# Top-k attention followed by a GELU MLP: the first MLP block over two slots, whole blocks from slot 12 on, and another order of the first loads

## The chip, the cores and the metric

The kernel runs on one core of one Trainium2 chip. A core has five engines that run side by side, each with its own stream of instructions: TensorE (matmuls; PE in the profile, with PEld for the loads of its stationary operand), VectorE (DVE), ScalarE (ACT), GpSimd (POOL) and SyncE (SP, which here only issues transfers). The metric is device time in microseconds (us), the median of several runs.

## The reference

```python
# q, k, v: (8, 8, 576, 64): 8 batches, 8 heads, 576 rows, 64 columns
scores = q @ k^T / sqrt(64)
kth    = 32nd largest score of each row
scores = where(scores >= kth, scores, -1e9)
attn   = softmax(scores)                 # over what is left; 1e-9 in the denominator
x      = (attn @ v), heads side by side  # (4608, 512)
out    = gelu(x @ w_in) @ w_out          # w_in (512, 2048), w_out (2048, 512), exact GELU
```

All of it is fp32.

## The kernel before

Two heads make a *pair*; 128 rows of a pair make an *item* (a last item of each two pairs takes the 64 rows that are left of each). There are 144 items. The main loop has a *slot* for each: in slot n the kernel starts the scores of item n+2, works on the softmax of item n-1, on the transposes of item n-2, on the product with v of item n-3, and searches the 32 largest of each row of item n.

```python
ahead = N + 4                                   # N = 144
for n in range(ahead):
    left[0] = 7 if START < n < START + 2 * NP else 8     # START = 10, NP = 4: pieces of the MLP in this slot
    weights_add(unit_in(n))                     # GpSimd: second half of a weight conversion
    scores(n + 2)                               # TensorE, and evictions by ScalarE
    product = attend(n - 3)                     # TensorE: attn @ v for two items, in every second slot
    late = n > START
    mlp(1)                                      # one piece, if its tokens are ready and left[0] > 0
    tr = transposes(n - 2)                      # TensorE, and copies by ScalarE
    ...
    softmax(n - 1, 0)                           # ScalarE: Prelu, then Exp with its sum, first half
    mlp(1)
    if not late:
        softmax(n - 1, 1)
    mlp(1)
    ...                                         # pieces between the transposes and those of later q and k
    if late:
        softmax(n - 1, 1)
    add_small(n - 1)                            # GpSimd: den + 1e-9
    ...
    run_gelus()
    mlp(left[0])                                # the pieces that are left
    run_gelus()
    if n < N:
        top_k(n, {3: lambda: inverse(n - 1)})   # VectorE: 4 rounds of MAX8 and MATCH_REPLACE8; 1/den at its end
    threshold(n)                                # GpSimd
    u = unit_in(n + 1)
    normalise(n - 1, 0 if u not in words else 2 if on_pool(u) else 1)  # halves done by VectorE, the others by GpSimd
    weights_size(unit_in(n + 1))                # ScalarE: first half of a weight conversion
    if n >= FIRST:
        load_weights(n + 2)
```

The MLP runs in *pieces*: L1 (x @ w_in) and L2 (gelu @ w_out), eight pieces to a *block* of two units, L1 and L2 blocks in turn. A unit of L1 fills one PSUM buffer, of which there are two; GELU empties it. The two GELUs of an L1 block are put in line after its last piece (first block) or after the sixth piece of the L2 block that follows, and run at the next `run_gelus`, at the latest ahead of the first piece of an L1 unit.

```python
def l1_piece(u, x):
    ...
    if x == 0:
        run_gelus()
    for ko in range(part * KO // m, (part + 1) * KO // m):
        nc.tensor.matmul(h_tile(u)[:, i, :], lhsT=w_in_sb[...], rhs=xT[...], ...)

GELU_AT = 5
pieces += behind(block(0, True), 7, (0, 1)) + block(2, True)
for u in range(2, NU, 2):
    pieces += behind(block(u - 2, False), GELU_AT, (u, u + 1))
    if u + 2 < NU:
        pieces += block(u + 2, True)
```

The weights come in as doubles whose words are converted to fp32 on the chip, in 16 units, one in a slot (the last two are a slot apart): two or three ScalarE operations of 128x1024 elements, and two or three of GpSimd. Units that fall in a slot before `START` take three on ScalarE, those from `START` on take their third on GpSimd (`on_pool`). Where a unit is converted, VectorE takes one or both halves of the normalisation from GpSimd.

```python
ORDER = [0, 1, 2, 3, 8, 9, 4, 5, 10, 11, 6, 7, 12, 13, 14, 15]
FIRST = 1
START = 2 * NP + 2
WARM = 16
SLOT_OF = {u: FIRST + i + (i == UNITS - 1) for i, u in enumerate(ORDER)}
```

The start: memsets, first loads, matmuls that only keep TensorE busy (`warm`), then the transposes of the first two pairs and the scores of items 0 and 1.

```python
for n, ts in raws.items():
    for t in ts[: 1 if n == "v" else 2]:
        (nc.vector if n == "v" else nc.gpsimd).memset(t[:, NM], 0.0)
make_identity(nc, ident)
for t in raws["v"][1:]:
    nc.gpsimd.memset(t[:, NM], 0.0)
...
load("k", 0, nc.scalar, nc.gpsimd)     # main part by ScalarE's queue, the 64 last rows by GpSimd's
load("q", 0)                           # all others by SyncE's queue
load("k", 1)
load("q", 1)
for n in range(2):
    load_weights(FIRST + n)
idle = raws["v"][0][:, NM].rearrange("p e d -> p (e d)")
warm = ps.tile([P, 512], f32, tag="l1", name="warm")
for _ in range(WARM):
    nc.tensor.matmul(warm[:, 0:P], lhsT=idle, rhs=idle, start=True, stop=True)
for pair in range(2):
    for piece in transpose_qk(pair, pair == 0):
        piece()
    if pair == 0:
        scores(0)
        scores(1)
```

The eviction of an item's scores, in `scores(i)`:

```python
nc.scalar.activation(spread(s, S + TL, SM), s_ps, func=AF.Copy, scale=scale)        # 128 x 1024
nc.scalar.activation(s[:, SM : S + TL], t_ps[:, 0:P], func=AF.Copy, scale=scale)    # 128 x 128
```

Of the kernel before, what the change touches and what calls it, by code (L numbers as in the profile page):

```python
# [14 lines left out]
def kernel(  # L15
# [19 lines left out]
    nc = tc.nc  # L35
    f32, i32, u32 = mybir.dt.float32, mybir.dt.int32, mybir.dt.uint32
    bf16, i16, u16 = mybir.dt.bfloat16, mybir.dt.int16, mybir.dt.uint16
    AF = mybir.ActivationFunctionType
    ALU = mybir.AluOpType

    B, H, S, D = q.shape
    P = 128
# [3 lines left out]
    NP = H // 2  # L46
    NM = S // P
    SM = NM * P
    TL = S - SM
# [6 lines left out]
    scale = 1.0 / float(D) ** 0.5  # L56
# [8 lines left out]
    ident = const.tile([P, P], f32, name="ident")  # L65
# [4 lines left out]

    raws = {n: [const.tile([P, NJ, 2, D], f32, name=f"raw_{n}{i}") for i in range(m)]
            for n, m in (("k", 2), ("q", 2), ("v", NP + 1))}
    for n, ts in raws.items():
        for t in ts[: 1 if n == "v" else 2]:
            (nc.vector if n == "v" else nc.gpsimd).memset(t[:, NM], 0.0)
    make_identity(nc, ident)
    for t in raws["v"][1:]:
        nc.gpsimd.memset(t[:, NM], 0.0)


    n_pairs = B * NP
# [2 lines left out]
    def raw_of(n, pair):  # L84
        return raws[n][pair % len(raws[n])]

    def load(n, pair, queue=None, queue2=None):
        if pair >= n_pairs:
            return
        queue = queue or nc.sync  # L90
        queue2 = queue2 or queue
        b, h0 = pair // NP, 2 * (pair % NP)
        t, src = raw_of(n, pair), sources[n]
        for e in range(2):
            queue.dma_start(
                out=t[:, 0:NM, e, :], in_=src[b, h0 + e, 0:SM].rearrange("(t p) d -> p t d", p=P)
            )
            queue2.dma_start(out=t[e * TL : (e + 1) * TL, NM, e, :], in_=src[b, h0 + e, SM:S])

# [18 lines left out]


    ORDER = [0, 1, 2, 3, 8, 9, 4, 5, 10, 11, 6, 7, 12, 13, 14, 15]
    FIRST = 1
    START = 2 * NP + 2
    WARM = 16
    words = {}
    low = const.tile([P, 1], f32, name="low")
    nc.gpsimd.memset(low, -EXP0 * 2.0**19)
# [3 lines left out]

    SLOT_OF = {u: FIRST + i + (i == UNITS - 1) for i, u in enumerate(ORDER)}
    UNIT_IN = {n: u for u, n in SLOT_OF.items()}
    unit_in = UNIT_IN.get
# [29 lines left out]
    def parts(u):  # L165

        t, dst = words[u], weights_of(u)[3].bitcast(i32)
        return t[:, :, 0::2], t.bitcast(mybir.dt.int16)[:, :, 2::4], t[:, :, 1::2].bitcast(i32), dst

    def weights_size(u):  # L170
        if u not in words:
            return
        w, first, below, d = parts(u)
        nc.scalar.activation(d, first, func=AF.Relu, bias=low, scale=2.0**19)

        nc.scalar.activation(below, first, func=AF.Prelu, bias=high, scale=2.0**-21, alpha=2.0**40)
        if not on_pool(u):
            nc.scalar.activation(w.bitcast(i32), w.bitcast(u32), func=AF.Copy, scale=2.0**-13)

    def on_pool(u):  # L180

        return SLOT_OF[u] >= START
# [3 lines left out]
    def weights_add(u):  # L186
        if u in words:
            w, _, below, d = parts(u)
            if on_pool(u):
                nc.gpsimd.tensor_scalar(  # L190
                    w.bitcast(i32), w.bitcast(u32), 2.0**-13, None, op0=ALU.mult
                )
            nc.gpsimd.tensor_tensor(d, d, below, op=ALU.add)
            nc.gpsimd.tensor_tensor(d, d, w.bitcast(i32), op=ALU.add)
        made.add(u)
# [53 lines left out]
    def spread(t, step, n):  # L249

        return bass.AP(tensor=t.tensor, offset=t.offset, ap=[list(t.ap[0]), [step, 2], [1, n]])

    def half(r, e):


        return slice((r ^ e) * TL, ((r ^ e) + 1) * TL)
# [5 lines left out]
    def scores(i):  # L262
        if i >= N:
            return
        pair, t = items[i]
        S_of[i] = s = work.tile([P, 2 * S], f32, tag="s", bufs=5, name="s")
        s_ps = ps.tile([P, 2, 512], f32, tag="s", bufs=1, name="s_ps")
        t_ps = ps.tile([P, 512], f32, tag="tp", name="t_ps")
        if t < NM:
            qk = qk_of[pair]  # L270
            lhsT = qk[:, t * P : (t + 1) * P]
            nc.tensor.matmul(t_ps[:, 0:P], lhsT=lhsT, rhs=qk[:, SM + P : KT], start=True, stop=True)  # L272
            for c in range(2):
                for e in range(2):
                    rows = slice(e * D, (e + 1) * D)
                    nc.tensor.matmul(  # L276
                        s_ps[:, e, c * 256 : (c + 1) * 256], lhsT=lhsT[rows, :],
                        rhs=qk[rows, KT + c * 256 : KT + (c + 1) * 256], start=True, stop=True,
                    )
            nc.scalar.activation(spread(s, S + TL, SM), s_ps, func=AF.Copy, scale=scale)  # L280
            nc.scalar.activation(s[:, SM : S + TL], t_ps[:, 0:P], func=AF.Copy, scale=scale)  # L281
        else:
            for r in range(2):
                qk = qk_of[pair + r]
                for e in range(2):
                    nc.tensor.matmul(
                        t_ps[half(r, e), r * TL : (r + 1) * TL],
                        lhsT=qk[:, SM + e * TL : SM + (e + 1) * TL],
                        rhs=qk[:, SM + P + e * TL : SM + P + (e + 1) * TL],
                        start=True, stop=True,  # L290
                    )

            for r in range(2):
                qk = qk_of[pair + r]
                for e in range(2):
                    rows = slice(e * D, (e + 1) * D)
                    nc.tensor.matmul(  # L297
                        s_ps[half(r, e), r, :], lhsT=qk[rows, SM + e * TL : SM + (e + 1) * TL],
                        rhs=qk[rows, KT:], start=True, stop=True,
                    )  # L300
            s2 = s.rearrange("p (r n) -> p r n", r=2)
            nc.scalar.activation(s2[:, :, 0:SM], s_ps, func=AF.Copy, scale=scale)
            nc.scalar.activation(
                s2[:, :, SM:S], t_ps[:, 0:P].rearrange("p (r n) -> p r n", r=2),
                func=AF.Copy, scale=scale,
            )
# [44 lines left out]
    def add_small(i):  # L351
        if i < 0 or i >= N:
            return
        st = stat_of[i]
        nc.gpsimd.tensor_scalar(st["den"], st["den"], 1e-9, None, op0=ALU.add)  # L355
# [224 lines left out]
    ready, left = [0], [0]  # L580
    staging = ExitStack()
    stage = staging.enter_context(tc.tile_pool(name="stage", bufs=1))

    load("k", 0, nc.scalar, nc.gpsimd)
    load("q", 0)
    load("k", 1)
    load("q", 1)
    for n in range(2):
# [10 lines that stand above are left out]
        if pair == 0:  # L599
            scores(0)  # L600
            scores(1)

# [10 lines left out]
    ahead = N + 4  # L615
    for n in range(ahead):

        left[0] = 7 if START < n < START + 2 * NP else 8
        weights_add(unit_in(n))
        scores(n + 2)  # L620
        product = attend(n - 3)
        late = n > START
        mlp(1)
        tr = transposes(n - 2)
        if product and n > START and done[0] < len(pieces) and pieces[done[0]][0] > ready[0]:

            for piece in tr[:1]:
                piece()
            tr, ready[0] = tr[1:], n_tok[0]
        softmax(n - 1, 0)  # L630
# [4 lines that stand above are left out]
        prep = prep_in.pop(n, [])  # L635
        if len(prep) > 1 and len(tr) == 3:
            tr, prep = tr[:1] + prep[:1] + tr[1:], prep[1:]
        for piece in tr[:-1]:
            piece()
            ready[0] = n_tok[0]  # L640
            mlp(1)
        ready[0] = n_tok[0]
        if late:
            softmax(n - 1, 1)
        add_small(n - 1)
        for piece in tr[-1:] + prep:
# [4 lines that stand above are left out]
        mlp(left[0])  # L651
        run_gelus()
        if n < N:
            top_k(n, {3: lambda: inverse(n - 1)})
        else:
            inverse(n - 1)
        threshold(n)
        u = unit_in(n + 1)

        normalise(n - 1, 0 if u not in words else 2 if on_pool(u) else 1)  # L660

        weights_size(unit_in(n + 1))
        if n >= FIRST:
            load_weights(n + 2)
        if n <= NP:
            load("v", n)
# [38 lines left out]
```

## Time and profile before

| | before |
|---|---|
| median of 3 runs | 1654.69 us (1654.48 to 1655.39) |
| profiled execution, first to last instruction | 1653.7 us |
| VectorE's first MAX8 (search of item 0) | 13.09 us |
| start of the search of items 10 and 11 | 115.87 and 126.64 us |
| start of the search of item 18 | 209.82 us |
| slowest of its instructions, in total: MAX8 and MATCH_REPLACE8 | 1152 and 864 of about 0.74 us each |
| GpSimd's normalisation of one half, 128x576 | 1.72 us |

The profile is that of one execution. Its page gives the busy time of each engine, then the span in 40 equal slices with a digit for the busy tenths, then the transfers, the chain of work that ended last, and the costliest groups. A line of a group, or of the instructions in order of time, names the engine, the line of the kernel, the operation, and output and inputs by the program's names; in square brackets stands how long the engine had been idle before it, and what released it. A slot has no mark in the profile; it can be told on TensorE by its score matmuls (`t_ps`, then `s_ps`), and on VectorE by the first MAX8 on `s`. An fp32 matmul shows as two instructions, a transpose as one.

### The profile page before, as it was taken

To read this page: it belongs to the slowest core of one execution; us is meant where nothing else is said; L and a number is where in the kernel's file an instruction comes from. 1 tells how busy PE (TensorE), PEld (TensorE's weight loads), DVE (VectorE), ACT (ScalarE), POOL (GpSimd) and SP (SyncE) were. 2 spreads that over 40 slices of the span, in tenths; PEclk is the share of its full clock that TensorE was granted. 3 is DMA by queue.
4 is the path that set the end of the run, shared out by engine and by line. 5 is a ranking of instruction groups with operands and counts; after the bars stand their busy time and mean duration, and the time that the engine had idled before them with its cause. 6 is when DMAs were issued, how large, how long until landed. Compare 5 with 4: busy or idle time off the path is not lost.

```text
span 1653.7 us, 25056 instructions
## 1 busy us (share of the span) xinstructions
PE 1593.8 (96%) x8832; PEld 1080.5 (65%) x8832; DVE 1419.6 (86%) x3049; ACT 1184.1 (72%) x2131; POOL 650.5 (39%) x756
## 2 busy tenths in 40 slices
PE   6669999999999999999999999999999999999999
PEld 4346566766666667676666667676666666666665
DVE  7999899989999889998989988998889898999800
ACT  6888777777777777777777777777777777777720
POOL 3677543333333333333333333333333333333300
PEclk7669999999999999999999999999999999999999
DMA  6423210011101111011110111001110001000000
GB/s 165 139 98 102 83 43 1 14 29 29 50 1 28 30 30 28 1 28 36 29 28 1 42 29 43 1 14 28 44 35 1 27 15 34 2 14 4 4 13 13
DMA packets 126621, 56.14 MB, mean 34 GB/s; under 512 B 117760, under 2 KB 117792, under 8 KB 126496
## 3 DMA queue, kind: packets, MB, share of 16 engines
q1 hardware_dynamic: 125376, 54.25, 12.2%
q8 instruction: 70, 1.15, 0.3%
q14 instruction: 55, 0.45, 0.1%
q10 hardware_dynamic: 1056, 0.26, 0.1%
q0 software_dynamic: 64, 0.03, 0.0%
HBM read 45.08 MB, written 9.44 MB: 33 GB/s over the span
## 4 chain that ended last, share of the span: by engine, by line
PE 92%; ACT 6%; DVE 1%; issue 1%; POOL 0%; ACTq 0%; POOLq 0%; DVEq 0%
PE h_ps L495 30%; PE y_ps L531 30%; PE o L443 9%; PE s_ps L276 8%; PE tp L412 8%; PE tp_qk L231 2%; PE t_ps L272 2%; ACT s L363 1%; PE o L454 1%; ACT s L362 1%; PE s_ps L297 1%; PE tp_t L394 1%; ACT s L280 1%; POOL s L375 0%; PE warm L595 0%
## 5 line engine op out<-in xcount | busy, mean ns | idle before, releaser
L323 DVE MAX8 top<-rest 128x8 f32<-128x576 f32 x864 | 608.9, 746 | 0.0
L495 PE MATMUL h_ps<-xT,w_in_sb 128*128 128x256 f32 (+1 forms) x2560 | 554.5, 362 | 3.8 <-ACT g L506 3.8
L531 PE MATMUL y_ps<-w_out_sb,g 128*128 128x512 f32 x1152 | 549.5, 599 | 0.0
L495 PEld LDWEIGHTS h_ps<-xT,w_in_sb 128*128 128x128 f32 x2560 | 429.6, 191 | 66.6 <-issue 19.6
L375 POOL TENSOR_SCALAR s<-s,rden 128x576 f32<-128x576 f32 x266 | 456.0, 1723 | 0.8 <-issue 0.4
L326 DVE MATCH_REPLACE8 rest<-top,rest 128x576 f32<-128x576 f32 x576 | 423.0, 741 | 0.0
L355 POOL TENSOR_SCALAR den<-den 128x2 f32<-128x2 f32 x144 | 32.0, 222 | 835.2 <-ACT s L363 834.4
L531 PEld LDWEIGHTS y_ps<-w_out_sb,g 128*128 128x128 f32 x1152 | 195.1, 190 | 166.8 <-issue 165.0
L280 ACT ACTIVATE s<-s_ps 128x1024 f32<-128x1024 f32 x128 | 131.5, 1027 | 167.3 <-PE s_ps L276 149.1
L363 ACT ACTIVATE s<-s,bias 128x576 f32<-128x576 f32 x288 | 223.3, 776 | 13.3 <-ACT s L362 0.7
L362 ACT ACTIVATE s<-s,neg 128x576 f32<-128x576 f32 x288 | 223.9, 778 | 0.3 <-POOL neg L338 0.2
L419 ACT COPY pt<-tp 128x512 f32<-128x512 f32 x256 | 147.1, 574 | 103.0 <-PE tp L412 103.0
L412 PEld LDWEIGHTS tp<-ident,s 128*128 128x128 f32 x1152 | 145.9, 144 | 111.9 <-issue 59.1
L326 DVE MATCH_REPLACE8 rest<-top,s 128x576 f32<-128x576 f32 x288 | 211.6, 742 | 0.0
L323 DVE MAX8 top<-s 128x8 f32<-128x576 f32 x288 | 201.8, 742 | 3.9 <-ACT s L281 3.9
L412 PE MATMUL tp<-ident,s 128*128 128x128 f32 x1152 | 178.6, 279 | 23.6 <-ACT pt L395 22.0
L443 PE MATMUL o<-pt,raw_v 128*64 128x256 f32 x1280 | 155.5, 390 | 0.0
L276 PE MATMUL s_ps<-qk 64*128 64x256 f32 x1024 | 153.9, 421 | 0.7 <-ACT s L280 0.7
L349 DVE RECIPROCAL rden<-den 128x2 f32<-128x2 f32 x144 | 23.0, 160 | 142.1 <-POOL den L355 141.8
L443 PEld LDWEIGHTS o<-pt,raw_v 128*64 128x64 f32 x1280 | 87.8, 139 | 66.2 <-issue 23.4
L276 PEld LDWEIGHTS s_ps<-qk 64*128 64x128 f32 x1024 | 92.5, 195 | 23.7 <-issue 1.6
L506 ACT ACTIVATE g<-h_ps 128x512 f32<-128x512 f32 x144 | 78.6, 595 | 34.0 <-PE h_ps L495 33.2
(66 smaller groups left out, 1088.3 us busy)
## 6 DMA issues: line engine op xcount, KB each, us to landing
raw_q<-in_q_dram SPq DMA_DIRECT2D x64, 128.0 KB, 2.4
raw_v<-in_v_dram SPq DMA_DIRECT2D x64, 128.0 KB, 2.5
out_dram<-y SPq DMA_DIRECT2D x32, 256.0 KB, 2.1
w_out_sb<-in_moe_w_in_dram SPq DMA_DIRECT2D x16, 511.8 KB, 4.9
raw_k<-in_k_dram SPq DMA_DIRECT2D x62, 128.0 KB, 2.5
w_out_sb<-in_moe_w_out_dram SPq DMA_DIRECT2D x10, 511.8 KB, 3.9
words<-in_moe_w_out_dram SPq DMA_DIRECT2D x6, 511.8 KB, 4.5
raw_q<-in_q_dram SPq DMA_DIRECT2D x64, 16.0 KB, 2.3
```

What stands on the lines that cost most here:

```text
L276: nc.tensor.matmul(s_ps[:, e, c * 256 : (c + 1) * 256], lhsT=lhsT[rows, :], rhs=qk[rows, KT + c * 256 : KT + (c + 1) * 256], start=True, s ...
L280: nc.scalar.activation(spread(s, S + TL, SM), s_ps, func=AF.Copy, scale=scale)
L323: nc.vector.max(st["top"][:, e, 8 * r : 8 * r + 8], cur[e])
L326: nc.vector.match_replace(rest[:, e], st["top"][:, e, 8 * r : 8 * r + 8], cur[e], LOWEST)
L362: nc.scalar.activation(s, s, func=AF.Prelu, bias=st["neg"][:, e, 1:2], scale=1.0, alpha=STEEP)
L363: nc.scalar.activation(s, s, func=AF.Exp, bias=st["bias"][:, e : e + 1], scale=1.0, accum_out=st["den"][:, e : e + 1],)
L375: (nc.vector if e >= 2 - on_dve else nc.gpsimd).tensor_scalar(s, s, st["rden"][:, e : e + 1], None, op0=ALU.mult)
L412: nc.tensor.transpose(tp[:, j * P : (j + 1) * P], s[:, first + j * P : first + (j + 1) * P], ident)
L419: nc.scalar.copy(out=dst, in_=tp.rearrange("p (j n) -> p j n", j=NM))
L443: nc.tensor.matmul(o[e * D : (e + 1) * D, 0:n], lhsT=vt[:, j, e, :], rhs=pt[:, e * NM + j if j < NM else 2 * NM, :], start=(j == 0), stop= ...
L495: nc.tensor.matmul(h_tile(u)[:, i, :], lhsT=w_in_sb[:, ko, f * P : (f + 1) * P], rhs=xT[:, ko, c0 : c0 + n], start=(ko == 0), stop=(ko == ...
L531: nc.tensor.matmul(y_of[sub], lhsT=g_of[u][:, i, sub * P : (sub + 1) * P], rhs=w_out_sb[:, f, :], start=(f == 0), stop=(f == FT - 1),)
```

## The change

The first L1 block of the MLP, which could run whole in slot 10, is spread over slots 10 and 11, four pieces in each; from slot 12 on each slot has eight pieces, so that a slot holds one whole block (before, seven pieces in slots 11 to 17). The conversion of the weights begins in slot 0 instead of slot 1, so each of the 16 units is there a slot earlier. At the start, the first k load is issued ahead of GpSimd's other work, most memsets go to VectorE, the first loads stand ahead of the identity's making, the warm-up has 9 matmuls instead of 16, and the scores of item 0 are evicted by ScalarE and VectorE together. The aim is an earlier first search, and slots that begin with a block of the MLP.

```diff
-    for n, ts in raws.items():
-        for t in ts[: 1 if n == "v" else 2]:
-            (nc.vector if n == "v" else nc.gpsimd).memset(t[:, NM], 0.0)
-    make_identity(nc, ident)
-    for t in raws["v"][1:]:
-        nc.gpsimd.memset(t[:, NM], 0.0)
+    nc.gpsimd.memset(raws["k"][0][:, NM], 0.0)
+    for t in raws["v"][:1] + raws["q"] + raws["k"][1:] + raws["v"][1:]:
+        nc.vector.memset(t[:, NM], 0.0)
@@ after the definition of load()
+    load("k", 0, nc.scalar, nc.gpsimd)
+    load("q", 0)
+    make_identity(nc, ident)
@@
-    FIRST = 1
+    FIRST = 0
     START = 2 * NP + 2
-    WARM = 16
+    WARM = 9
@@ scores(i)
+            if i == 0:
+                nc.scalar.activation(s[:, 0:SM], s_ps[:, 0], func=AF.Copy, scale=scale)
+                nc.vector.tensor_scalar(s[:, SM : S + TL], t_ps[:, 0:P], scale, None, op0=ALU.mult)
+                nc.vector.tensor_scalar(s[:, S + TL :], s_ps[:, 1], scale, None, op0=ALU.mult)
+                return
@@ ahead of the first transposes
-    load("k", 0, nc.scalar, nc.gpsimd)
-    load("q", 0)
     load("k", 1)
@@ behind the first transposes
             scores(0)
             scores(1)
+    weights_size(unit_in(FIRST))
@@ the main loop
-        left[0] = 7 if START < n < START + 2 * NP else 8
+        left[0] = 4 if n in (START, START + 1) else 8
```

## The prediction

> **What bounds the kernel now.** I read the page first (shares and slices), then cut the span into stages, then asked for the waits of the stage in which an engine is idle, and last for the instructions in order of time at the two places that the change touches.
>
> ```profile
> PE 1593.8 (96%) x8832; PEld 1080.5 (65%) x8832; DVE 1419.6 (86%) x3049; ACT 1184.1 (72%) x2131; POOL 650.5 (39%) x756
> ...
> PE   6669999999999999999999999999999999999999
> ...
> PEclk7669999999999999999999999999999999999999
> ```
>
> TensorE has the largest share, but the slices show two regimes: the first three slices (about 120 us) are not full, all others are. The stages in numbers (columns: span, length, busy us and instructions of PE, PEld, DVE, ACT, POOL, granted clock, DMA share, GB/s):
>
> ```profile
> 0.00:13.10 13.10, 10.11 (x56) 8.95 (x58) 1.20 (x4) 3.06 (x4) 3.37 (x19) 1.00 0.68 177
> 13.10:112.00 98.90, 58.42 (x276) 37.03 (x276) 98.40 (x211) 85.50 (x141) 63.15 (x53) 0.66 0.46 134
> 112.00:206.80 94.80, 86.46 (x467) 56.92 (x468) 84.67 (x183) 76.71 (x127) 64.47 (x47) 0.96 0.30 92
> 206.80:215.00 8.20, 5.16 (x38) 3.34 (x37) 8.20 (x20) 5.12 (x12) 5.23 (x6) 1.00 0.01 2
> 215.00:1586.00 1371.00, 1370.91 (x7793) 934.85 (x7791) 1227.15 (x2636) 1006.38 (x1837) 514.29 (x633) 1.00 0.09 22
> 1586.00:1653.70 67.70, 62.79 (x212) 39.39 (x208) 0.00 (x0) 7.29 (x13) 0.00 (x0) 0.99 0.04 16
> ```
>
> The reader is to see four things. Up to 13.1 us VectorE does almost nothing: it waits for the first scores. From 13.1 to 112 us (slots 0 to 9) VectorE is busy 98.40 of 98.90 us: the top-k search sets the pace. From 112.0 us, where TensorE takes up slot 10, to 215 us (early in slot 18) neither is full. From 215 to 1586 us TensorE is busy 1370.91 of 1371.00 us. So the end of the kernel is "the moment at which TensorE stands where it stands at 215 us" plus a fixed amount of matmul work; a gain must come from ahead of that moment, out of the first 13.1 us or the 103 us of the third and fourth row. The waits of 112 to 215 us (us in total, times, longest):
>
> ```profile
> DVE rden L349 <- POOL den L355: 9.4, 5, 4.0
> ...
> PE tp L412 <- ACT pt L395: 3.8, 3, 1.5
> ...
> PE tp_t L399 <- POOL s L375: 3.0, 2, 1.6
> ...
> PE h_ps L495 <- ACT g L506: 2.7, 1, 2.7
> ```
>
> VectorE stands 9.4 us in five slots before the reciprocal, because the softmax of the item before comes late from ScalarE. TensorE's largest single wait is a matmul that wants a PSUM buffer which GELU hasn't emptied (2.7 us). After it the matmuls run at half speed for a while: four h_ps instructions take 1.74 us at 180.77 us, against 1.03 us elsewhere. In order of time at the start of the span:
>
> ```profile
> 1.04 6.67 PE L595 MATMUL warm<-raw_v 128*128 128x128 f32 x32 [1.04 <-DVE raw_v L75]
> ...
> 2.73 1.26 POOL L98 DMA_DIRECT2D raw_k<-in_k_dram  x2
> ...
> 7.55 0.60 PE L231 MATMUL tp_qk<-ident,raw_k 128*128 128x128 f32 x4
> ...
> 11.86 1.02 ACT L280 ACTIVATE s<-s_ps 128x1024 f32<-128x1024 f32 x1 [1.65 <-PE s_ps L276]
> 12.78 0.27 ACT L281 ACTIVATE s<-t_ps 128x128 f32<-128x128 f32 x1
> ...
> 13.09 1.42 DVE L323 MAX8 top<-s 128x8 f32<-128x576 f32 x2 [3.88 <-ACT s L281]
> ```
>
> The first transposes have no wait before them: they follow the warm-up matmuls at once, so the warm-up, not the data, sets 7.55 us. The path then runs through copies and score matmuls to one ScalarE eviction after the other and the first MAX8 at 13.09 us.
>
> **What the Trainium skill says.** "TensorE: Matmul & The Clock Gate", Part 1: TensorE starts at half clock, is released after a busy window of about 3.4 us, throttled again after an idle one, and the windows run freely. The trace agrees: a warm-up instruction of 128 columns takes about 0.23 us up to 7 us and 0.11 us later (the clock record says 1.00 all that time, so the durations decide), and the clock falls to 0.50 at 18 to 20 us. "ScalarE: Activation LUTs", What ACT_TABLE_LOAD costs: about 1.28 us for each change of table set, plus a drain. The trace has 1.28 us for each, one into GELU and one back to Exp per pair of GELUs. "DMA: Bandwidth & Descriptors", Anatomy of one DMA: about 2 us of fixed cost. The trace has 2.1 us at least, and a median of 2.4 us for q and 3.2 us for the k loads of ScalarE's queue.
>
> **The change, part by part.**
>
> *Pieces of the MLP.* A piece is two L1 matmuls of 256 columns (4 instructions) or one L2 matmul of 512 (2 instructions): 0.86 to 0.87 us either way. First I count what moves. Before: the 32 h_ps instructions of slot 10 are 8 pieces, slots 11 to 16 have 7 each, slot 17 has 6 and then finds its next tokens not ready: 8 + 6x7 + 6 = 56. After: 4 + 4 + 6x8 = 56. So no piece leaves the tail of the kernel. What changes is where blocks begin: from slot 12 on each slot holds one block of 8, and GELUs fall at the end of a slot instead of into its middle.
>
> *Gain in slots 10 to 18, two ceilings.* VectorE: its own period is 10.77 us in a slot that normalises both halves there (115.87 to 126.64 us) and about 9.8 us in one that doesn't (9.65 us from first to second search, plus 0.15 us of reciprocal). With the weight units one slot earlier, slots 14, 16 and 17 leave normalisation to GpSimd (before: 15 and 17), 5x10.77 + 3x9.8 = 83.2 us, against the 93.95 us from 115.87 to 209.82 us in which they took place: at most 10.7 us. TensorE: of 103.0 us it is busy 91.6 us; about 4.5 us of those are half clock (slot 10 up to 118 us, and slot 15), so 87 us of work. Slots 10 and 11 become light (2x1.4 scores + 2.3 attend + 8x0.87 pieces + 3 us of transposes = 15 us) and wait for VectorE. Slot 12's first transposes need the normalised row at 137.4 us (115.87 + 2x10.77), and 1.4 + 2.3 + 0.9 us of work lies ahead of them, so slot 12 starts at about 133 us on the old clock. 133 + (87 - 15) = 205 instead of 215: at most 10 us.
>
> *What of it is lost again.* GpSimd's normalisation of both halves takes 3.43 us. After search 14 it ends near 172.8 us, and TensorE is ready for it near 170.5 us, because slot 15 has no attend: 2.3 us. Slots 12, 14 and 16 now hold 6.9 us of pieces, 2.3 us attend, 1.4 us scores, about 1.7 us transposes, 12.3 us against VectorE's 10.8 us; every second slot makes one engine wait for the other, and ScalarE still pays 2.56 us of table loads for each pair of GELUs. I allow 2 us for that. 10 - 4.5 = 5.5 us gained.
>
> *Start.* GpSimd has one memset ahead of its k loads instead of more than ten small instructions; its load starts near 1.0 us instead of 2.73 us, so the tails land near 4.9 us instead of 6.6 us. Warm-up: 18 instructions x 0.22 us end near 5.0 us. First transposes near 5.2 us instead of 7.55 us: 2.35 us. The split eviction replaces 1.02 + 0.27 us by about 0.8 us: 0.45 us. Against it: with a warm-up of 4 us the clock may not be released when the transposes come. Ten transposes at half clock add about 0.7 us on the path, eight score instructions 0.9 us (2.08 us at 17.87 us against 1.14 us at 10.68 us). Gain 2.8 us when warm, 1.2 us when cold; I take 2.0 us. This passes undiminished through slots 0 to 9, which VectorE bounds.
>
> *Weights from slot 0 on.* One conversion (1.25 + 1.22 + 1.14 us on ScalarE) now comes ahead of slot 0, into the 2.9 us in which ScalarE waits at 17 us. After it ScalarE is about where it was at 25 us; the softmax of item 0 ended 2.7 us before VectorE needed it, of which 2 us are eaten by the earlier start. No cost expected.
>
> Sum: -5.5 - 2.0 = -7.5 us, 1654.7 to **1647.2 us**.
>
> **The rivals.**
> 1. *TensorE takes VectorE's place at once.* Seven pieces were chosen to leave room; with eight, slots 12 to 17 average over 11 us and the 9.4 us of VectorE's waits merely become TensorE's own work. For it: both ceilings are within 1 us of each other. Against it: the 2.7 us buffer wait and the 3.0 us wait in slot 18 come from the broken alignment and from ScalarE's late chain. It would leave 2 us of the middle: 1650.5 us.
> 2. *The start is not earlier.* The clock stays low for another window, or the weight words, whose loads took up to 7.2 us, reach ScalarE late and delay the first softmax. Against it: the words are issued no later than before. It would leave the middle alone: 1649 us; with a stall that reaches VectorE, 1652 us.
> 3. *All falls into place.* No wait is left in slots 12 to 18 and the start is warm: -10 - 2.8: 1642 us.
>
> **Range and chances.** Rivals 1 and 2 together give 1652.5 us, rival 3 about 1642 us; the working lies between. 8 times in 10: **1641.5 to 1652.5 us**. 2% is 33 us, more than all idle time ahead of 215 us outside of VectorE's stage, so faster by over 2%: 0.01; within 2%: 0.985; slower by over 2%: 0.005 (only if a wait appeared in each of the 126 later slots).
>
> **What would show it.** First MAX8 at 10.3 to 11.9 us instead of 13.09 us, with score matmuls of 1.1 us (warm) or 2.1 us (cold). Slots 1 to 9 still at 10.27 us on VectorE. In slots 10 to 18, VectorE's wait for the denominator down from 9.4 us to under 4 us and no wait of a matmul for GELU over 1 us. TensorE full from slot 18 on, and from there to the end the same time as before: from the last score matmul ahead of 208.17 us to the end 1445.5 us. I am wrong if the search of item 18 starts (209.82 us before) less than 3 us or more than 13 us earlier, or if idle time shows up after slot 18.

## The result, and the profile after

| | before | changed |
|---|---|---|
| median of 6 runs each | 1655.12 us (1654.48 to 1656.36) | 1647.91 us (1646.15 to 1649.69) |
| ratio | | 0.9956, 95% interval 0.9943 to 0.9969 |
| first MAX8 | 13.09 us | 10.75 us |
| start of the search of item 10 | 115.87 us | 114.24 us |
| TensorE takes up slot 10, 12, 18, 19 | 112.02, 137.85, 206.79, 221.82 us | 113.02, 134.00, 202.85, 214.57 us |
| from slot 19 on TensorE to the end | 1431.8 us | 1431.8 us |

The predicted total, 1647.2 us, came out within 0.7 us. The stages tell where it came from (span, length, busy us of PE, PEld, DVE, ACT, POOL, clock, DMA share, GB/s; the changed kernel):

```profile
0.00:10.75 10.75, 7.72 (x40) 6.31 (x40) 3.07 (x13) 2.46 (x3) 2.49 (x12) 1.00 0.63 140
10.75:113.00 102.25, 59.03 (x276) 37.90 (x276) 101.15 (x217) 89.26 (x144) 68.46 (x55) 0.69 0.51 150
113.00:202.83 89.83, 86.27 (x466) 56.41 (x467) 84.39 (x183) 75.99 (x128) 61.09 (x47) 0.95 0.27 84
...
208.20:1578.70 1370.50, 1370.41 (x7789) 933.90 (x7789) 1226.65 (x2635) 1005.98 (x1837) 514.30 (x633) 1.00 0.09 22
```

The last row and the last line of the table say that nothing changed from slot 19 on: TensorE is as full as before, for as long. The 7.25 us lie ahead of it. But look where: the first MAX8 is 2.3 us earlier, and yet TensorE takes up slot 10 a microsecond *later* than before. All of the gain appears between slot 10 and slot 19: slots 10 and 11 take 20.98 us where they took 25.83, slots 12 to 17 take as long as before (68.9 us) with seven more pieces in them, and slot 18 takes 11.72 us where it took 15.03. The waits of that stretch, 113 to 216 us of the changed kernel (us in total, times, longest):

```profile
DVE rden L356 <- POOL den L362: 5.6, 5, 2.3
...
PE tp L419 <- ACT pt L402: 1.9, 2, 1.4
...
PE t_ps L273 <- ACT pt L426: 1.6, 2, 1.4
```

VectorE's wait for the denominator is 5.6 us where it was 9.4. The matmul that waited for GELU (2.7 us) and the transposes of slot 18 that waited for GpSimd (3.0 us) are gone from the list. The start, in order of time:

```profile
1.04 4.21 PE L600 MATMUL warm<-raw_v 128*128 128x128 f32 x18 [1.04 <-DVE raw_v L75]
...
5.17 0.63 PE L232 MATMUL tp_qk<-ident,raw_k 128*128 128x128 f32 x4
...
9.51 0.60 ACT L283 ACTIVATE s<-s_ps 128x512 f32<-128x512 f32 x1 [1.65 <-PE s_ps L277]
...
10.14 0.69 DVE L285 TENSOR_SCALAR s<-s_ps 128x512 f32<-128x512 f32 x1 [1.41 <-ACT s L283]
...
10.75 1.41 DVE L330 MAX8 top<-s 128x8 f32<-128x576 f32 x2
```

The transposes begin at 5.17 us, as predicted, and at full clock. The whole lead over before comes from here. The split eviction adds nothing: VectorE's half starts at 10.14 us, only when ScalarE's half has ended, and from the first eviction to the MAX8 it takes 1.24 us, where it took 1.23 us (11.86 to 13.09).

### The profile page after: what moved, and what is told of

It is laid out like the page before. It is cut to its first block, busy times and chain, and to the rows that moved or that the text cites. A ratio compares the mean times of both kernels' runs of the same rounds, so it can differ in the third digit from the quotient of the medians.

```text
span 1646.4 us, 25031 instructions
## 1 busy us (share of the span) xinstructions
PE 1591.6 (97%) x8818; PEld 1077.6 (65%) x8818; DVE 1420.6 (86%) x3056; ACT 1185.0 (72%) x2131; POOL 649.9 (39%) x750
## 3 DMA queue, kind: packets, MB, share of 16 engines
q8 instruction: 70, 1.15, 0.3%
## 4 chain that ended last, share of the span: by engine, by line
PE 93%; ACT 3%; DVE 1%; SPq 1%; POOL 1%; DMA 0%; issue 0%; ACTq 0%; DVEq 0%; POOLq 0%
PE y_ps L538 31%; PE h_ps L502 30%; PE o L450 9%; PE s_ps L277 8%; PE tp L419 8%; PE tp_qk L232 2%; PE t_ps L273 2%; PE o L461 1%; ACT s L370 1%; PE s_ps L304 1%; PE tp_t L401 1%; ACT s L369 1%; DVE top L330 1%; DVE rest L333 1%; SPq L95 0%
```

## The experiments

Each time is a median, each ratio is to the kernel before in the same set of runs. "Slot 12" is when TensorE starts its score matmuls of that slot in the profile. The times are of several executions, the moments of one profile each. How far a moment moves by itself can be seen from before, left_only, heavy10 and misaligned: their code is the same up to slot 10, and TensorE takes up slot 10 at 112.02, 110.34, 111.68 and 110.55 us. From slot 19 to the end all fourteen profiles take 1431.8 to 1431.9 us.

| run | start | weights from | pieces in slots 10, 11, 12 to 17 | time, us | ratio (95%) | first MAX8 | slot 12 | slot 19 |
|---|---|---|---|---|---|---|---|---|
| before | old | slot 1 | 8, 7, 7 (slot 17: 6) | 1655.12 | | 13.09 | 137.85 | 221.82 |
| changed | new | slot 0 | 4, 4, 8 | 1647.91 | 0.9956 (0.9943 to 0.9969) | 10.75 | 134.00 | 214.57 |
| start_only | new | slot 1 | 8, 7, 7 | 1655.21 | 1.0001 (0.9992 to 1.0009) | 10.84 | 138.02 | 221.74 |
| left_only | old | slot 1 | 4, 4, 8 | 1646.54 | 0.9948 (0.9933 to 0.9963) | 11.70 | 132.13 | 212.27 |
| left_first | old | slot 0 | 4, 4, 8 | 1648.07 | 0.9958 (0.9942 to 0.9975) | 12.28 | 134.14 | 214.72 |
| start_first | new | slot 0 | 8, 7, 7 | 1654.38 | 0.9995 (0.9986 to 1.0003) | 11.52 | 137.32 | 220.09 |
| start_left | new | slot 1 | 4, 4, 8 | 1648.33 | 0.9953 (0.9939 to 0.9967) | 10.60 | 133.92 | 214.70 |
| heavy10 | old | slot 1 | 8, 0, 8 | 1652.77 | 0.9983 (0.9976 to 0.9990) | 12.99 | 137.43 | 219.36 |
| misaligned | old | slot 1 | 4, 8, 8 (slot 17: 4) | 1658.14 | 1.0019 (1.0011 to 1.0027) | 11.82 | 136.65 | 225.36 |
| left_relief | old | slot 1 | 4, 4, 8 | 1645.27 | 0.9937 (0.9923 to 0.9951) | 12.79 | 131.31 | 211.62 |
| start_left_relief | new | slot 1 | 4, 4, 8 | 1643.75 | 0.9928 (0.9914 to 0.9942) | 11.20 | 129.54 | 210.31 |
| left_fill | old | slot 1 | 4, 4, 8 | 1645.15 | 0.9940 (0.9922 to 0.9957) | 12.59 | 130.72 | 211.43 |
| start_left_fill | new | slot 1 | 4, 4, 8 | 1644.27 | 0.9930 (0.9914 to 0.9946) | 11.05 | 131.41 | 211.55 |
| after_fill | new | slot 0 | 4, 4, 8 | 1645.16 | 0.9939 (0.9923 to 0.9955) | 11.43 | 129.56 | 211.69 |

### The three parts one by one

*start_only*: the changed kernel with the weights and the pieces as they were before.

```diff
-    FIRST = 0
+    FIRST = 1
...
-    weights_size(unit_in(FIRST))
...
-        left[0] = 4 if n in (START, START + 1) else 8
+        left[0] = 7 if START < n < START + 2 * NP else 8
```

> The kernel before with only the new start (order of loads and memsets, 9 warm-up matmuls, item 0's split eviction); weights from slot 1 and seven pieces a slot as before. Theory A (the start's gain passes through the slots that VectorE bounds): first MAX8 near 10.8 us, search of item 10 about 2.3 us earlier than 115.9 us, time 1652.5 to 1653.3 us. Rival B (the start's gain runs into the waits of slots 12 to 17 and is lost there): first MAX8 as early, but the search of item 18 within 1 us of 209.8 us and the time over 1654 us.

Measured 1.0001 (0.9992 to 1.0009): the new start alone is worth nothing, as rival B had it. TensorE and VectorE at slots 10 to 12, first the score matmuls of slot 10, then the reciprocal ahead of the search of item 12 (in brackets: idle time before, and what ended it):

```profile
111.95 0.80 PE L273 MATMUL t_ps<-qk 128*128 128x128 f32 x2 [0.25 <-ACT pt L426]
...
137.71 0.17 DVE L356 RECIPROCAL rden<-den 128x2 f32<-128x2 f32 x1 [3.58 <-POOL den L362]
```

The search of item 10 starts at 113.62 us, 2.25 us earlier than before. TensorE takes up slot 10 at 111.95 us, where it was 112.02. What VectorE had gained it gives back at once: it stands 3.58 us before this reciprocal, 1.17 us in the kernel before. So the loss isn't in slots 12 to 17 alone, as the rival said, but has been there since before slot 10. On TensorE the lead over the kernel before is 1.96 us at slot 0, 1.54 at slot 1, 1.15 at slots 2 to 4, and gone at slot 7. In slot 0 it runs into a transfer: the transposes of the third pair's k can't start before its load has landed, and they start at 18.7 to 19.0 us in thirteen of the fourteen profiles, with the old start as with the new (19.88 us in the kernel before). In start_only:

```profile
18.82 1.09 PE L232 MATMUL tp_qk<-ident,raw_k 128*128 128x128 f32 x4 [2.06 <-DMA raw_k<-in_k_dram]
```

In slot 9 the loss can be watched. TensorE's transposes in the kernel before, and then in start_only:

```profile
107.00 0.48 PE L394 MATMUL tp_t<-ident,s 128*128 128x128 f32 x1 [2.72 <-POOL s L375]
...
110.23 1.12 PE L412 MATMUL tp<-ident,s 128*128 128x128 f32 x4 [1.90 <-ACT pt L395]
```

```profile
104.75 0.33 PE L401 MATMUL tp_t<-ident,s 128*128 128x128 f32 x1 [1.04 <-POOL s L382]
106.82 1.12 PE L419 MATMUL tp<-ident,s 128*128 128x128 f32 x4 [1.74 <-ACT s L288]
110.16 1.11 PE L419 MATMUL tp<-ident,s 128*128 128x128 f32 x4 [2.23 <-ACT pt L402]
```

The row that VectorE and GpSimd hand over is there 2.25 us earlier (104.75 against 107.00 us). The transposes after it wait for ScalarE, which is no earlier: its softmax of this slot starts at 106.66 us, and at 106.74 us in the kernel before.

*left_only*: the kernel before with one line changed.

```diff
-        left[0] = 7 if START < n < START + 2 * NP else 8
+        left[0] = 4 if n in (START, START + 1) else 8
```

> The kernel before with only the new rule for the pieces (4, 4, then 8). Theory A (the blocks' alignment takes away the mid-slot GELUs and the waits behind them): 4 to 5 us of the 5.6 us that the middle gained, so 1650 to 1651 us, VectorE's wait for the denominator in slots 10 to 18 down from 9.4 us to 4 to 6 us. Rival C (it is the weights one slot earlier that free slots 12 to 17): 0 to 1.5 us, 1653.5 to 1655 us.

0.9948 (0.9933 to 0.9963): the one line gives the whole gain, about 8.6 us, more than the 4 to 5 that theory A expected. Rival C falls. The waits on VectorE up to slot 18 shrink to one, 1.65 us before the search of item 17.

*left_first*: left_only, with `FIRST = 0` and the conversion ahead of slot 0.

> The kernel before with the new rule for the pieces and the weights from slot 0 on, old start. Theory A: the whole middle gain, 5.6 us, 1649.5 us, 1 us more than the rule alone, as one slot less normalises on VectorE (0.95 us). Rival C: also 5.6 us, but 4 us or more beyond the rule alone.

*start_first*: the changed kernel with the old line for the pieces.

> The changed kernel with the old rule for the pieces (seven in slots 11 to 17). Theory A: start's gain plus about 1 us, 1651.5 to 1652.5 us, and the 2.7 us wait of a matmul for GELU is there again. Rival C: nearly the whole gain, 1648 to 1649.5 us.

0.9958 (1648.07 us) and 0.9995 (1654.38 us). start_first meets neither expectation; in it the matmul that waits for GELU is there again (2.6 us), as theory A had said. The earlier weights add nothing that can be measured to the rule, and neither do both other parts together without it. The intervals of left_only, left_first and the changed kernel overlap, so it can't be said whether the earlier weights and the new start cost something.

### What in the rule matters: light slots, or whole blocks

The edits are shown against left_only.

```diff
 heavy10
-        left[0] = 4 if n in (START, START + 1) else 8
+        left[0] = 0 if n == START + 1 else 8
 misaligned
-        left[0] = 4 if n in (START, START + 1) else 8
+        left[0] = 4 if n == START else 8
```

> The kernel before with eight pieces in slot 10, none in slot 11, then eight a slot: whole blocks from slot 12 on, as with four and four, but slot 10 heavy. Theory F (what counts is that each slot from 12 on holds one whole block): as the rule alone, 1646 to 1648 us. Theory G (what counts is that slots 10 and 11 are light, so that ScalarE's evictions and softmax of item 10 aren't behind two GELUs): VectorE's wait of 1.2 us in slot 11 comes back, slot 12 begins near 136 us, 1649.5 to 1651 us.

> The kernel before with four pieces in slot 10 and eight in each later one: slot 10 light, but each slot from 11 on holds the end of one block and the start of the next, until the pieces run out in slot 17. Theory F: a matmul waits for GELU again for 2 us or more in the middle of a slot, 1649.5 to 1652 us. Theory G: 1646 to 1648 us.

Both theories are half right, and both times fall outside of all four ranges. heavy10 has whole blocks and loses 6.2 us against left_only; misaligned has a light slot 10 and loses 11.6 us, 2.5 us more than the kernel before takes. Waits between 113 and 216 us, first heavy10:

```profile
DVE rden L349 <- POOL den L355: 7.1, 4, 2.7
...
PE tp L412 <- ACT s L281: 2.6, 1, 2.6
```

then misaligned:

```profile
DVE rden L349 <- POOL den L355: 12.4, 6, 3.5
PE h_ps L495 <- ACT g L506: 7.8, 3, 2.7
...
PE tp_t L399 <- POOL s L375: 3.0, 2, 1.6
```

In heavy10 TensorE's transposes of slot 11 wait for ScalarE, and slot 12 starts at 137.43 us, as late as before the change (the theory had said 136). In misaligned three L1 units begin in the middle of a slot and each waits 2.6 to 2.7 us for its PSUM buffer, because GELU stands in ScalarE's queue behind half a softmax, two copies and a table load. A second table load then stands ahead of that softmax's last Exp (each 1.28 us), and VectorE, which needs its sum, waits 12.4 us in all. misaligned differs from left_only in more than the alignment: it has four pieces more in slot 11 and four fewer in slot 17. The three waits for GELU come to 7.8 us; how the 11.6 us divide isn't shown.

### What holds slots 1 to 9

Theory D, formed after start_only: ahead of slot 10 a ring of ScalarE and TensorE is as slow as VectorE. Six runs on it.

*start_left*: the changed kernel with `FIRST = 1`, and without the conversion ahead of slot 0.

> The changed kernel with the weights from slot 1 on again (new start, new rule for the pieces). Theory D (ahead of slot 12 a chain of ScalarE and TensorE sets the pace, in which ScalarE has no gap; one more conversion of three operations, 3.6 us, ahead of slot 10 lengthens it): TensorE takes up slot 12 1.5 to 2.5 us earlier than the 134.0 us of the changed kernel, time 1646 to 1646.8 us. Rival E (VectorE sets the pace there, as predicted): slot 12 at the same time, and 1647.9 us or more, as VectorE normalises in one slot more.

1648.33 us, slot 12 at 133.92 us against 134.00: the earlier weights cost nothing here, so theory D's number for them was wrong (and rival E's number fits).

*left_relief* and *start_left_relief*: left_only and start_left without ScalarE's third operation on each unit of slots 1 to 9, whose low words are then left out of the result; GpSimd's second addition goes to a place that isn't read.

```diff
-        if not on_pool(u):
-            nc.scalar.activation(w.bitcast(i32), w.bitcast(u32), func=AF.Copy, scale=2.0**-13)
...
-            nc.gpsimd.tensor_tensor(d, d, w.bitcast(i32), op=ALU.add)
+            if on_pool(u):
+                nc.gpsimd.tensor_tensor(d, d, w.bitcast(i32), op=ALU.add)
+            else:
+                nc.gpsimd.tensor_tensor(w.bitcast(i32), d, below, op=ALU.add)
```

> The kernel before with the new rule for the pieces, and without ScalarE's third operation (1.14 us) on each weight unit of slots 1 to 9; the low words of these weights are left out of the result, GpSimd's work is the same. Theory D: slot 12 begins 2 us or more ahead of the 132.1 us of the run with that operation, time 1644 to 1645 us. Rival E: slot 12 and the time within 0.5 us.

> As the run before, with the new start. Theory D: with ScalarE relieved VectorE sets the pace of slots 1 to 9, so the new start's 1 to 2 us now reach slot 12 and the end: 1 to 2 us less than without the new start. Rival E: the same difference as between the two kernels that have the operation.

TensorE takes up slot 12, in left_relief:

```profile
131.31 0.49 PE L273 MATMUL t_ps<-qk 128*128 128x128 f32 x2 [1.39 <-ACT pt L420]
```

and in start_left_relief:

```profile
129.54 0.49 PE L274 MATMUL t_ps<-qk 128*128 128x128 f32 x2 [1.39 <-ACT pt L427]
```

With ScalarE relieved the new start does reach slot 12 (1.8 us) and the end: 1645.27 (1644.71 to 1645.35) to 1643.75 us (1643.46 to 1643.92), 1.5 us, the 1.6 us by which the first MAX8 is earlier in these two profiles. With the operation in place the new start gave nothing (start_only against before, start_left against left_only). That is theory D's difference, and not rival E's. What ScalarE waits for between TensorE's slots 1 and 10 shows why. In start_only, and in the kernel before, all of its waits there end with TensorE. With the relief some end with the threshold that follows a search; first left_relief, then start_left_relief:

```profile
ACT s L363 <- POOL neg L339: 4.2, 3, 1.9
```

```profile
ACT s L370 <- POOL neg L346: 3.4, 3, 1.9
```

In both of these TensorE takes up slot 10 5.7 us ahead of VectorE's search of item 10, in none of the other twelve more than 4.2 us ahead: here VectorE sets that moment. The old start gained only 0.8 us at slot 12 from the relief, not 2; its first search came at 12.79 us in this profile, at 11.70 us in left_only.

*start_left_fill*, *left_fill*, *after_fill*: three idle matmuls of 128 columns at each place in slots 1 to 9 at which the MLP would have a piece later; they use the PSUM buffer of L2, which is free until slot 13.

```diff
+    fill_ps = ps.tile([P, DM], f32, tag="l2", name="fill")
...
     def mlp(n):
+        if n == 1 and 1 <= slot[0] < START:
+            for _ in range(3):
+                nc.tensor.matmul(fill_ps[:, 0:P], lhsT=ident, rhs=ident, start=True, stop=True)
+            return
...
+        slot[0] = n
```

> As the run before, with three idle matmuls of 128 columns at each place in slots 1 to 9 where later a piece of the MLP stands, so that TensorE's clock stays high. Theory D: the transposes and scores that ScalarE waits for take half the time, ScalarE's repeated 0.7 us waits for them shrink to 0.3 us, slot 12 begins 2 to 4 us earlier than without, until VectorE sets the pace: 1643.5 to 1645 us. Rival E: no change, or 1 to 2 us longer, as the idle matmuls stand ahead of real ones.

> The new rule for the pieces and the idle matmuls of slots 1 to 9, with the old start and the weights from slot 1 on. If the start's gain reaches the end once TensorE's clock is high: 1645.3 to 1646.3 us, 1 to 2 us more than the same with the new start (1644.3 us). If it is the clock alone: 1644.3 us.

> The changed kernel with the idle matmuls of slots 1 to 9. Theory D, in which the earlier weights cost ScalarE time: 0.5 to 2 us more than with the weights from slot 1 on (1644.3 us), but at least 1.5 us less than the changed kernel. If the earlier weights are free: 1643.5 to 1644.5 us.

40 to 70 us, first start_left, then start_left_fill:

```profile
40.00:70.00 30.00, 18.51 (x77) 11.32 (x75) 29.73 (x66) 25.49 (x40) 21.57 (x17) 0.56 0.49 142
```

```profile
40.00:70.00 30.00, 25.52 (x192) 22.12 (x191) 29.89 (x66) 26.71 (x43) 21.70 (x18) 0.92 0.52 151
```

The third last column is the clock: 0.56 becomes 0.92. Slot 12 begins at 131.41 instead of 133.92 us, and the time is 1644.27 instead of 1648.33 us, the lowest of a kernel that computes everything. That is theory D's number, but not by its path. TensorE's way from slot 1 to slot 10 takes 93.34 us without the idle matmuls and 93.22 us with them, so here the ring isn't faster; slot 10 begins only 0.4 us earlier (112.95 and 112.52 us). The other 2.1 us are gained in slot 10 itself. Its scores and its product with v, first start_left, then start_left_fill:

```profile
113.68 2.08 PE L277 MATMUL s_ps<-qk 64*128 64x256 f32 x8
115.69 3.33 PE L450 MATMUL o<-pt,raw_v 128*64 128x256 f32 x20
```

```profile
113.09 1.13 PE L277 MATMUL s_ps<-qk 64*128 64x256 f32 x8
114.15 2.38 PE L450 MATMUL o<-pt,raw_v 128*64 128x256 f32 x20
```

With idle matmuls ahead of it, slot 10 has these at full clock. In the other two pairs the times fall by 1.4 us (left_only to left_fill) and 2.8 us (changed to after_fill). Slots 10 and 11 together get shorter in all three pairs, by 2.1, 2.9 and 1.5 us; slot 10 itself begins 0.4 us earlier, 1.5 us later and 2.9 us earlier, so whether the ring gains isn't shown. The three kernels with idle matmuls lie within 0.9 us, with overlapping ranges, so what the new start or the earlier weights are worth beside them stays open.

## Why the prediction was right or wrong

**The total was right because two terms were off in opposite directions.** The sum was -5.5 (pieces) - 2.0 (start). Alone, the pieces give -8.6 us (0.9948) and the start 0.1 us (1.0001). That the total came within 0.7 us is luck.

**The step that failed** is "This passes undiminished through slots 0 to 9, which VectorE bounds". VectorE was indeed busy all the time, and the first MAX8 came as early as predicted (10.75 us; 10.3 to 11.9). VectorE even carried its lead to the search of item 10 (2.25 us in start_only). But a full engine is not yet the one that sets the end. TensorE can take up slot 10 only after ScalarE has gone through the evictions, softmax, copies and conversions of the slots before, and in start_only that ring of ScalarE and TensorE reached slot 10 at 111.95 us, where it was 112.02. In the kernel before the two were about even: in its profile and the three others with the same code up to there, slot 10 comes 98.6 to 98.9 us after the first MAX8, whether that is at 11.70 or at 13.09 us. In the four profiles with the new start and without relief or idle matmuls it comes 100.0 to 102.4 us after. So there was little room for a lead of 2 us. Why the ring takes between 90.8 and 93.3 us from slot 1 to slot 10, from profile to profile, stays open. The row of 13 to 112 us could have warned me: ScalarE was busy 85.50 us beside VectorE's 98.40. I read only the column that was full.

**The allowance of 4.5 us for new waits was too large.** The 2.3 us for GpSimd's normalisation in slot 15 didn't occur. I had put one piece ahead of a slot's first transposes, where the loop has three. The changed kernel in slot 15:

```profile
171.39 2.84 PE L538 MATMUL y_ps<-w_out_sb,g 128*128 128x512 f32 x6
174.07 0.27 PE L401 MATMUL tp_t<-ident,s 128*128 128x128 f32 x1
```

Six y_ps instructions are three pieces, 2.6 us, and the transpose after them has no wait: GpSimd ended at 173.31 us. With one piece ahead TensorE would have been ready near 172.3 us (my estimate, from 171.39 us and 0.9 us for a piece), so even then the wait would have been about 1 us.

**Slot 12's start** was put at 133 us with the old start, 17.1 us after the search of item 10. It came 17.6 us after that search with the rule alone (132.13 us) and 19.8 us after it in the changed kernel (134.00 us).

**The split eviction** was put at 0.45 us and gave nothing; the transposes' 2.35 us came out as 2.38 us (7.55 to 5.17). The last rows of the first k landed at 5.95 us before, not at 6.6, and at 5.06 us in the changed kernel.

**The tail** was to begin in slot 18. From the last score matmul of slot 18 to the end it took 1445.4 us before and 1442.1 us in the changed kernel: 3.3 us of the gain lie in slot 18 itself, where the transposes had waited 3.0 us for GpSimd. Only from slot 19 on is it the same.

**What held:** 56 pieces before and after, so from slot 19 on nothing changed; the search of item 18 7.4 us earlier, between 3 and 13; the GELU wait gone; TensorE full from slot 18 on but for one wait of 1.2 us at the end; searches of slots 1 to 9 still 10.27 to 10.34 us apart, but for one of 10.96 us; "no cost" of the earlier weights, within the noise. VectorE's waits fell to 5.6 us, not under 4; what that cost isn't shown, but TensorE was busy 86.27 of 89.83 us beside them. Rival 1, TensorE at once in VectorE's place, was true of slots 12 to 17 as a description (68.9 us for them before and after), but not as a loss. Rival 2, no earlier start, had the right size for the start's term, but for the wrong reason: the first MAX8 was earlier.

## What to carry to other kernels

An engine that is full in a stage need not be the one that hands work on to the next stage. Before counting an earlier start as a gain, follow the moment at which the next stage's own engine takes over, here TensorE at slot 10, and ask which engine that moment waits for. In a loop of slots, giving each slot one whole block, so that the operation that frees a buffer falls on a slot's end, was worth 8.6 us against seven pieces a slot, and 11.6 us against eight a slot shifted by half a block, a rule that also fills slot 11 more.

## What the runs showed of the hardware

The same start doesn't take the same time. With the old start the first MAX8 came between 11.70 and 13.09 us in seven profiles. The warm-up is the cause: in all seven the MAX8 starts 5.4 us after its end. Its 32 instructions took 6.67 us in the kernel before, and in left_only

```profile
1.04 5.28 PE L595 MATMUL warm<-raw_v 128*128 128x128 f32 x32 [1.04 <-DVE raw_v L75]
```

This fits what the Trainium skill says in "TensorE: Matmul & The Clock Gate", Part 1, that the clock's windows run freely and the release depends on where the first matmul falls in one. The page names a spread of 0.5 us either way; here it is wider, for in these seven the instructions became short between 4.15 and 6.96 us. With nine warm-up matmuls the first MAX8 came between 10.60 and 11.52 us: there the transposes start at 5.0 to 5.6 us, and in five of seven profiles they wait for the first k load instead. So of the 2.3 us by which the two profiles above showed the start earlier, the mean of the profiles leaves 1.4 us (12.5 to 11.1 us).

Idle matmuls ahead of real ones, in slots in which TensorE was idle for two fifths of the time, made the kernel 4.1 us shorter (1648.33 to 1644.27 us, in the same set of runs). At slot 12 the lead was 2.5 us, and 2.1 of these came from slot 10, whose matmuls then ran at full clock (score matmuls 1.13 us, before 2.08).
